# Attention and mixer kernel on one core: a fourth Strassen pair, earlier input sums, scores as two jobs, and a planner with new costs and rank offsets

## The chip, the cores and the metric

One NeuronCore of a Trainium2 chip runs the whole program in one launch. The metric is device microseconds of one execution. The kernel before took 565.9 us (median of 3 runs, 565.84 to 566.09). The execution that was profiled took 566.33 us.

## The reference

Causal attention over 4 batches, 12 heads, 448 positions and 64 channels a head, then a mixer on the attention's output, all in float32 (the weights come as float64):

```
x  = softmax(mask(q k^T / 8)) v            # 4 x 12 x 448 x 64, then 4 x 448 x 768
u  = x + (relu(x^T w_tok1) w_tok2)^T       # token mixing, 448 -> 256 -> 448
out = u + relu(u w_ch1) w_ch2              # channel mixing, 768 -> 1536 -> 768
```

Float32 accuracy is kept with split operands: each factor is held as a high and a low part, and a product is three matmuls (high by high, high by low, low by high).

## The kernel before, in words

The kernel first writes down jobs, then a planner (`Plan.emit`, L137) puts them into an order, and only that order is sent to the engines. A job has the engines that may do it with a cost in ns for each, the jobs that it needs, the buffers and PSUM banks that it holds, and a rank. The planner keeps a clock of its own: whenever an engine is free on that clock, it gets the ready job of the lowest rank whose buffers and banks are open; a job with a choice of engines goes where it would end first. Buffers of one name are a ring, and are given out strictly in the order in which the program asked for them. On the chip every engine then works through its list in order, and waits where a semaphore says so. When PE has nothing ready in the first 75 us of the planner's clock, a matmul without use (L602, the filler) is put in.

The stages:

1. Attention, by pairs of heads (24 pairs, 6 a batch). `load_pair` (L626) loads k, q and v with 11 DMA issues a pair. `prep` (L658) transposes k and q on VectorE into two `kq` buffers (five in all). `heads` (L672) has the scores as one PE job, `qk` (L689): 14 matmuls on 64 by 64 quarters of the array, 28 records in the trace, into four PSUM banks, which it and the four `prob` buffers have to be had together. Then come `low` (VectorE, minimum), `expo` (ScalarE), `guard` and `recip`, and `norm`. Pairs 0 to 11 turn the probabilities by PE (`by_tensor`, L759), pairs 12 to 23 by DMA (`by_dma`, L801), where `split` (L822) separates the 16-bit halves into the other `prob` buffer of each name. `values` (L863) multiplies with v on 128 by 64 halves of the array; `xturn` (L908) turns the result.
2. Token mixing, `tokens` (L959), in three parts a batch, with hidden values in `h1h` and `h1l` (one buffer each).
3. Channel mixing. The 1536 inner columns are 12 blocks of 128, in four quarters of three. `channels` (L1046) does one quarter for one or two batches: `up` (products with w_ch1), relu and its low part, then `down`, and `add` (L1120) puts the result onto `u` in place. `STAGES` (L274) says which quarter for which batches. A quarter for one batch is 108 matmuls of 448 columns. Batches 2 and 3 take blocks 3 to 8 together, in three pairs of blocks by Strassen's scheme: `mixtures` (L1152) makes four sums of the two batches' inputs for each of three row blocks, `combined` (L1247) makes the sums of the weights, and `group` (L1320) does the seven products, the sums of these, the relu and the downs. `mixtures` takes its buffers from attention once this is over; `combined` takes `u` buffers that earlier batches no longer need, and `wraw`.
4. `store` (L1490) turns a finished block of `u` on VectorE into a `kq` buffer and sends it with four DMA issues; `finish` (L1457) does the last block.

Before the change batches 2 and 3 already have quarter 0 added (for batch 2 in stage 4) when `mixtures` runs, so it has to rebuild batch 2's input from its two parts (`again`, L1210).

Of the kernel before, what the change touches and what calls it, by code (L numbers as in the profile page):

```python
# [19 lines left out]

class Slot:


    def __init__(self, ring):
        self.ring = ring
        self.index = ring.uses
        self.left = 0
        self.tile = None
        ring.uses += 1

    def take(self):
        self.ring.taken.append(self)
# [16 lines left out]
class Bank:  # L49


    def __init__(self, plan, kind, share):
        self.plan, self.kind, self.share = plan, kind, share
        self.left = 0
        self.bank = None

# [4 lines left out]
    def take(self):  # L61
        p = self.plan
        self.bank = p.banks.pop(0)
# [7 lines left out]
class Job:  # L71
    def __init__(self, order, costs, fn, rank, moved, lock=False):
        self.order, self.costs, self.fn, self.rank, self.moved, self.lock = order, costs, fn, rank, moved, lock
        self.waits = 0
        self.ready = 0.0
        self.after = []
        self.takes = []
        self.holds = []
# [4 lines left out]
class Plan:  # L83
# [7 lines left out]
    WINDOW, KEEP, WARM = 3400.0, 0.65, 75000.0  # L91
    LAG = {"pe": 230.0, "act": 150.0, "dve": 150.0, "pool": 150.0, "sp": 100.0}
    OWN = {"pe": 0.0, "act": 100.0, "dve": 130.0, "pool": 100.0, "sp": 100.0}
# [28 lines left out]
    def job(self, costs, fn, needs=(), holds=(), rank=0.0, moved=0.0, lock=False):  # L122

        j = Job(len(self.jobs), costs, fn, rank, moved, lock)
# [4 lines left out]
        for s in holds:  # L129
            if s.left == 0:  # L130
                j.takes.append(s)
            s.left += 1
# [4 lines left out]
    def emit(self):  # L137
        now = 0.0
        free = dict.fromkeys(self.ENGINES, 0.0)
        port = {"dve": 0.0, "pool": 0.0}  # L140
        dma = 0.0

        def until(j, e, t):
# [3 lines left out]
            return t + j.costs[e]  # L147
# [17 lines left out]
        while left:  # L165
# [3 lines left out]
            for e in self.ENGINES:  # L169
# [4 lines left out]
                while ready[e]:  # L174
# [4 lines left out]
                    open_ = all(s.open() for s in j.takes) and self.fits(j)  # L179
# [29 lines left out]
                end = until(pick, e, now)  # L209
                if e == "pool" or (e == "dve" and pick.lock):  # L210
                    port[e] = end
                free[e] = end
                if e == "pe":
                    self.spans.append((now, end))
                if pick.moved:
                    dma = end = max(end + 650.0, dma) + pick.moved
                    end += 800.0
                heapq.heappush(events, (end, 0, pick.order, pick))
# [25 lines left out]
def kernel(  # L244
# [72 lines left out]
    def act_ps(n):  # L317
        return 160.0 + 0.833 * n

    def act_sb(n):  # L320
        return 200.0 + 0.833 * n

    def dve1(n):
        return 150.0 + 1.04 * n

    def dve2(n):
        return 150.0 + 0.55 * n

    def pool1(n):
        return 230.0 + 0.85 * n  # L330

    def pool2(n):
        return 270.0 + 2.1 * n

    def pe(*ns):
        return sum(max(109.0, 0.458 * n) for n in ns)

    def move(n):
        return n / 290.0
# [45 lines left out]
    def narrow(n, shape, source, f, rank, needs=(), raw=None):  # L385
# [31 lines left out]
        j = plan.job({"sp": 520.0}, load, holds=[raw], rank=rank, moved=move(shape[0] * n * 8))  # L417
        j = plan.job({"act": act_sb(n)}, size, [j, *needs], [raw, f], rank)
# [5 lines left out]
    def token_weights():  # L424
        work = [(w_tok1, w1hi, w1lo, c, 0, DT) for c in range(NCH)]
        work += [(w_tok2, w2hi, w2lo, c, o, S // 2) for c in range(NM) for o in (0, S // 2)]
        for n, (src, hi, lo, c, o, w) in enumerate(work):
# [10 lines left out]
            a = narrow(w, [P, 1, w], source, f, TRANK, raw=slot(("wh", "wl")[n % 2]))  # L438
# [17 lines left out]
    def channel_weights(stage, o):  # L456
# [5 lines left out]
        size = P * NT * P * 4  # L462
        if stage < NQT:
            def source():
# [12 lines left out]
                {"sp": 520.0},  # L477
                lambda e: nc.sync.dma_start(out=scratch[m], in_=flat(f.tile)),
                got, [f], rank, moved=move(size),
            )  # L480
        else:
            got = [plan.job(
                {"sp": 520.0},
# [3 lines left out]
                [saved[m]], [f], rank, moved=move(size),  # L487
# [31 lines left out]
    def reread(sources, saves, rank):  # L519
# [7 lines left out]
        return f, plan.job({"sp": 520.0}, load, saves, [f], rank, moved=move(P * NT * P * 4))  # L527
# [37 lines left out]
    QUARTERS = ((0, 0, 6), (0, 1, 5), (1, 2, 4), (1, 3, 3), (0, 1, 1), (1, 3, 2), (1, 2, 0),  # L565
# [991 lines left out]
```

## Time and profile before

| | |
|---|---|
| median of 3 runs | 565.9 us |
| profiled execution | 566.33 us, of which span 564.6 us |
| PE busy | 548.2 us, 97% |
| DVE, ACT, POOL busy | 395.0, 304.7, 223.1 us |
| TensorE's granted clock | 1.00 in all 40 slices |
| chain that ended last | PE 90%, DMA issue queue of SP 3%, ACT 3%, DMA 2%, DVE 1% |
| filler matmuls (L602) | 55 |

The span is the time from the first to the last instruction; the rest of an execution's time lies around it. PE's busy time is a union of records whose ends are modelled, so a PE that looks busy can still have gaps between starts; distances between starts are the safer reading.

### The profile page before, as it was taken

Reading aid. Unit: us, or ns where it says so; the run is one execution under the profiler, and the core shown is the slowest. Engines: PE = TensorE matmul, PEld = TensorE weight load, DVE = VectorE, ACT = ScalarE, POOL = GpSimd, SP = SyncE. Lnnn points to the kernel's source line nnn. Section 1 sums busy time; section 2 is a strip of 40 time slices with the busy share of each in tenths; the row PEclk is TensorE's granted clock in tenths of the full one; section 3 lists DMA queues with packets and bytes.
Section 4 is the critical chain, followed back from the end, with each engine's and each line's share of the span. In section 5 each row is a group of like instructions: output and inputs, shape, how many; then the busy total and the mean of one; then the engine's idle time right before and its main releaser. Section 6 shows DMA issues by size and latency. Waiting matters only on the chain.

```text
span 564.6 us, 10295 instructions
## 1 busy us (share of the span) xinstructions
PE 548.2 (97%) x3512; PEld 473.5 (84%) x3512; DVE 395.0 (70%) x925; ACT 304.7 (54%) x746; POOL 223.1 (40%) x320
## 2 busy tenths in 40 slices
PE   8789999999999999999999999999999999999996
PEld 4467888878888988988988988988999998999995
DVE  4575868588777677778867687566576668677835
ACT  3678888787687566776667754674143120111010
POOL 2465675535352321430353621353356546232001
PEclk9999999999999999999999999999999999999999
DMA  6777647576988689789996766766221030312525
GB/s 112 157 154 149 155 104 174 161 180 150 197 224 190 149 203 204 177 222 200 217 217 132 151 111 122 148 126 127 62 74 56 29 111 2 111 55 86 126 57 99
DMA packets 230340, 77.37 MB, mean 137 GB/s; under 512 B 206544, under 2 KB 219024, under 8 KB 230288
## 3 DMA queue, kind: packets, MB, share of 16 engines
q1 hardware_dynamic: 217056, 74.99, 58.6%
q10 hardware_dynamic: 13232, 1.72, 1.8%
q8 instruction: 28, 0.46, 0.3%
q14 instruction: 24, 0.20, 0.1%
HBM read 49.15 MB, written 14.94 MB: 114 GB/s over the span
## 4 chain that ended last, share of the span: by engine, by line
PE 90%; SPq 3%; ACT 3%; DMA 2%; DVE 1%; issue 0%; POOL 0%; DVEq 0%; ACTq 0%
PE ps L1056 48%; PE ps L1444 8%; PE ps L882 7%; PE ps L1376 6%; PE ps L1007 5%; PE ps L974 5%; PE ps L695 5%; PE ps L781 3%; SPq L635 2%; PE ps L928 2%; DMA wl<-in_moe_w_tok_dram 1%; ACT prob L724 1%; SPq L400 1%; ACT pt L343 0%; DMA kq<-in_q_dram 0%
## 5 line engine op out<-in xcount | busy, mean ns | idle before, releaser
L1124 DVE TENSOR_TENSOR u<-ps,u 128x448 f32<-128x448 f32 x107 | 66.3, 622 | 47.1 <-PE ps L1056 33.6
L724 ACT ACTIVATE prob<-prob,stat 128x448 f32<-128x448 f32 (+6 forms) x168 | 84.0, 504 | 26.1 <-DVE stat L712 25.9
L345 POOL TENSOR_SCALAR prob<-prob,stat 128x448 f32<-128x448 f32 (+6 forms) x125 | 69.9, 572 | 39.7 <-DVE stat L746 36.7
L1056 PE MATMUL ps<-gh,wh 128*128 128x448 f32 x216 | 80.6, 373 | 0.0
L1056 PE MATMUL ps<-gh,wl 128*128 128x448 f32 x216 | 79.0, 366 | 0.0
L1056 PE MATMUL ps<-gl,wh 128*128 128x448 f32 x216 | 79.0, 366 | 0.0
L1056 PE MATMUL ps<-uh,wh 128*128 128x448 f32 x198 | 75.0, 379 | 0.0
L1056 PE MATMUL ps<-uh,wl 128*128 128x448 f32 x198 | 72.5, 366 | 0.0
L1056 PE MATMUL ps<-ul,wh 128*128 128x448 f32 x198 | 72.4, 366 | 0.0
L345 POOL TENSOR_SCALAR wh<-wf 128x768 fp32r<-128x768 f32 x27 | 23.1, 854 | 113.4 <-PE ps L1056 65.1
L712 DVE CUSTOM_DVE_ANT_0 prob<-ps,mask 128x448 f32<-128x448 f32 (+6 forms) x168 | 62.3, 412 | 0.3 <-PE ps L695 0.3
L743 POOL TENSOR_SCALAR stat<-stat 128x3 f32<-128x3 f32 (+1 forms) x43 | 13.3, 309 | 96.5 <-ACT prob L724 95.0
L882 PE MATMUL ps<-pt,vraw 128*64 128x448 f32 (+3 forms) x384 | 46.8, 386 | 1.4 <-ACT pt L343 1.4
L882 PEld LDWEIGHTS ps<-pt,vraw 128*64 128x64 f32 x384 | 25.4, 136 | 25.0 <-issue 14.0
L349 ACT COPY pt<-pt 128x512 uint16<-128x512 uint16 (+1 forms) x46 | 36.8, 875 | 15.5 <-DMA pt<-prob 15.4
L1056 PEld LDWEIGHTS ps<-gh,wh 128*128 128x128 f32 x216 | 40.6, 188 | 3.7
L1056 PEld LDWEIGHTS ps<-gl,wh 128*128 128x128 f32 x216 | 40.6, 188 | 3.5 <-DVE gl L1092 0.3
L1056 PEld LDWEIGHTS ps<-gh,wl 128*128 128x128 f32 x216 | 40.5, 188 | 3.2
L695 PEld LDWEIGHTS ps<-kq,kq 64*64 64x64 f32 x672 | 36.0, 132 | 8.3 <-issue 4.2
L695 PE MATMUL ps<-kq,kq 64*64 64x448 f32 (+6 forms) x672 | 41.8, 383 | 0.0
L354 DVE TENSOR_TENSOR wl<-wf,wh 128x768 fp32r<-128x768 f32 x35 | 35.9, 1033 | 8.5 <-ACT wh L343 4.9
L1056 PEld LDWEIGHTS ps<-uh,wh 128*128 128x128 f32 x198 | 37.2, 188 | 3.7
(144 smaller groups left out, 1224.2 us busy)
## 6 DMA issues: line engine op xcount, KB each, us to landing
wraw<-in_moe_w_ch_dram SPq DMA_DIRECT2D x24, 768.0 KB, 5.3
wf<-scratch SPq DMA_DIRECT2D x30, 384.0 KB, 3.2
scratch<-wf SPq DMA_DIRECT2D x24, 384.0 KB, 5.8
vraw<-in_v_dram SPq DMA_DIRECT2D x48, 96.0 KB, 2.4
out_dram<-kq SPq DMA_DIRECT2D x68, 56.0 KB, 1.8
kq<-in_k_dram SPq DMA_DIRECT2D x60, 56.0 KB, 3.9
kq<-in_q_dram SPq DMA_DIRECT2D x56, 56.0 KB, 2.5
gh<-in_k_dram SPq DMA_DIRECT2D x36, 56.0 KB, 2.3
```

Of the source, the lines that this page charges most:

```text
L345: eng[e].tensor_scalar(dst, src, scale, 0.0, op0=ALU.mult, op1=ALU.add)
L349: nc.scalar.copy(out, in_)
L354: eng[e].tensor_tensor(dst, a, b, op=ALU.subtract)
L695: nc.tensor.matmul(scores[r].tile[lanes, WHERE[c]:WHERE[c] + wide(c)], lhsT=qe.tile[LANES[j], c * QC:(c + 1) * QC], rhs=ke.tile[LANES[j], ...
L712: nc.vector.tensor_tensor_reduce(out=part(c, r), in0=ps.tile[:, WHERE[c]:WHERE[c] + wide(c)], in1=mask[:, S - wide(c):], scale=-SCALE, sca ...
L724: nc.scalar.activation(part(c, r), part(c, r), AF.Exp, bias=stat.tile[:, 0, AT[c]:AT[c] + 1], scale=-1.0, accum_out=stat.tile[:, 1, AT[c]: ...
L882: nc.tensor.matmul(ps.tile[LANES[j], c * QC:(c + nq) * QC], lhsT=s.tile[:, kb, j], rhs=view[:, o:o + nq, j], start=(kb == 0), stop=(n == 3),)
L974: nc.tensor.matmul(ps.tile[:, :PART], lhsT=w[:, c, m * P:(m + 1) * P], rhs=x.tile[:, c, :], start=(n == 0), stop=(n == len(work) - 1),)
L1056: nc.tensor.matmul(ps.tile[:, :S], lhsT=x.tile[:, at_:at_ + P], rhs=y, start=(n == 0 and i == 0), stop=(n + 1 == w[2] and i == 2),)
L1124: eng[e].tensor_tensor(u, ps.tile[:, :S], u, op=ALU.add)
L1376: nc.tensor.matmul(ps.tile[:, :S], lhsT=l()[:, t * P:(t + 1) * P], rhs=r, start=(t == 0 and n == 0), stop=(t == half - 1 and n == 2),)
L1444: nc.tensor.matmul(ps.tile[:, :S], lhsT=l.tile[:, t * P:(t + 1) * P], rhs=r.tile, start=(n == 0), stop=(n == 3 * len(fs) - 1),)
```

## The change

- **Strassen for a fourth pair.** Stage 5, quarter 3 (blocks 9, 10, 11) of batches 2 and 3, goes. Block 11 becomes a group of its own with plain products, and blocks 9 and 10 a pair by Strassen's scheme; both run ahead of the three pairs there were.
- **Sums of mixed inputs.** `mixtures` reads batch 2's and 3's `u` as the token mixing leaves it, so `again` goes, and every addition onto `u` of batches 2 and 3 now waits for the sums that read that block. The token weights' storage, free after the last token mixing, serves as further places for the sums; one `pt` buffer is given to the combined weights in place of a second `u` buffer.
- **Scores as two jobs**, one for two banks each, and with the 14 matmuls in another order: the two heads now alternate, head 0 on the upper and head 1 on the lower 64 rows of the array, both into the same bank.
- **Stores** use `h1h` and `h1l` instead of `kq`.
- **The planner**: costs of nearly all operations are changed; a DMA's time is modelled with a lead, a duration and the room in its ring; switching PE between quarters and the whole array costs 100 ns; from 30 us on the costs of ACT, DVE and POOL are taken 10% higher; transposes on PE don't count against the filler; and a table, `NUDGE`, adds an offset to the rank of 136 kinds of jobs (name and rank).

```diff
+NUDGE = {
+    "narrow.shift": {3.5: 18, 14: 6},
+    "token_weights.<lambda>": {3.5: -43},
+    "heads.expo": {0: 12, 2: -44, 10: 0.4, 12: 3, 14: -16, 24: 43, 26: 15, 32: 18.7, 44: 3},
+    "heads.<lambda>": {6: -19, 14: 38, 16: -43, 20: 17, 28: -7, 40: -10, 44: 3},
...
+    "group.down": {59.04: 9, 59.21: 14, 59.38: 45, 59.55: 5, 59.89: 12, 60.06: 5, 60.4: -8, 60.74: -19, 61.47: 3,
+        64.89: -8, 65.97: -6},
...
+}
-    WINDOW, KEEP, WARM = 3400.0, 0.65, 75000.0
-    LAG = {"pe": 230.0, "act": 150.0, "dve": 150.0, "pool": 150.0, "sp": 100.0}
+    LEAD, SWITCH, RING = 1400.0, 100.0, 128.0
+    SLACK, SETTLED = 1.1, 30000.0
+    WINDOW, KEEP, WARM = 3400.0, 0.7, 75000.0
+    LAG = {"pe": 200.0, "act": 145.0, "dve": 130.0, "pool": 80.0, "sp": 100.0}
...
+        rank = rank + NUDGE.get(name, {}).get(round(rank, 3), 0.0)
...
+                if e == "pe":
+                    end += self.SWITCH * (pick.tiled != tiled)
...
+                    while queued(e, end) + pick.ring > self.RING:
+                        end += 20.0
+                    start = max(now + self.LEAD, dma)
+                    dma = start + pick.moved
...
-    STAGES = ((0, (0,)), (1, (0, 1)), (2, (0, 1)), (3, (0, 1)), (0, (1, 2)), (3, (2, 3)), (0, (3,)))
+    STAGES = ((0, (0,)), (1, (0, 1)), (2, (0, 1)), (3, (0, 1)), (0, (1, 2)), (0, (3,)))
-    GROUPS = ((3, 4), (5, 6), (7, 8))
+    FIRST_GROUP = 5.0
+    SPAN = (0.34, 0.63)
+    GROUPS = ((11,), (9, 10), (3, 4), (5, 6), (7, 8))
...
     def act_ps(n):
-        return 160.0 + 0.833 * n
+        return 65.0 + 0.833 * n
...
-    QUARTERS = ((0, 0, 6), (0, 1, 5), (1, 2, 4), (1, 3, 3), (0, 1, 1), (1, 3, 2), (1, 2, 0),
-                (1, 1, 5), (1, 0, 6), (0, 3, 3), (0, 2, 4), (0, 3, 2), (0, 2, 0), (1, 1, 1))
+    QUARTERS = ((0, 0, 6), (1, 0, 6), (0, 1, 5), (1, 1, 5), (0, 1, 1), (1, 1, 1),
+                (0, 3, 3), (1, 3, 3), (0, 2, 4), (1, 2, 4), (0, 3, 2), (1, 3, 2), (0, 2, 0), (1, 2, 0))
...
-        holds = scores + probs + [ke, qe, stat]
-        m = plan.job({"pe": 1900.0}, qk, ready + [last_qk[0]], holds, rank)
-        last_qk[0] = m
+        made = {}
+        for rg, cost in zip(RG, (930.0, 740.0)):
+            holds = [x for r in rg for x in (scores[r], probs[r])] + [ke, qe, stat]
+            m = plan.job({"pe": cost}, lambda e, rg=rg: qk(e, rg), ready + [last_qk[0]], holds, rank, tiled=True)
+            last_qk[0] = m
+            made.update(dict.fromkeys(rg, m))
...
-                exps.append(plan.job({"act": 480.0 + 0.833 * wide(c)}, expo, [a], [probs[r], stat], rank))
+                exps.append(plan.job({"act": 277.0 + 0.857 * wide(c)}, expo, [a], [probs[r], stat], rank))
...
-        if b == B - 1:
-            ready.append(unmixed[t])
+        if b >= B - 2:
+            ready += unmixed[b, t]
...
-            p1, i1, e1 = again(t)
-            p2, i2, e2 = again(t + half)
-            x1, j1, f1 = mix("T1", t, p1, at(u3, t), ALU.subtract, [i1] + n3, [e1, u3])
-            mix("T3", t, p2, p1, ALU.subtract, [i1, i2], [e1, e2])
-            x2, j2, f2 = mix("T2", t, p2, x1, ALU.subtract, [i2, j1], [e2, f1])
-            x4, j4, f4 = mix("T4", t, at(u3, t + half), x2, ALU.subtract, [j2] + n3, [u3, f2])
-            unmixed[t], unmixed[t + half] = j1, j4
+            v = t + half
+            n2, m2, n3, m3 = u_whole[B - 2, t], u_whole[B - 2, v], u_whole[B - 1, t], u_whole[B - 1, v]
+            x1, j1, f1 = mix("T1", t, at(u2, t), at(u3, t), ALU.subtract, [n2, n3], [u2, u3])
+            _, j3, _ = mix("T3", t, at(u2, v), at(u2, t), ALU.subtract, [n2, m2], [u2])
+            x2, j2, f2 = mix("T2", t, at(u2, v), x1, ALU.subtract, [m2, j1], [u2, f1])
+            _, j4, _ = mix("T4", t, at(u3, v), x2, ALU.subtract, [m3, j2], [u3, f2])
+            unmixed[B - 2, t], unmixed[B - 2, v] = [j1, j3], [j2, j3]
+            unmixed[B - 1, t], unmixed[B - 1, v] = [j1], [j4]
...
-            spare.extend([slot("u"), slot("u"), slot("wraw")])
+            spare.extend([slot("u"), slot("pt"), slot("wraw")])
...
     def store(b, t, ready):
-        o = slot("kq")
+        o = slot(("h1h", "h1l")[t % 2])
...
-    for stage in range(len(STAGES) - 2):
+    mixtures()
+    for stage in range(len(STAGES) - 1):
         channels(stage)
-    mixtures()
-    channels(len(STAGES) - 2)
-    for number in range(len(GROUPS)):
-        group(number, 6.0 + number * 0.63)
+    at = FIRST_GROUP
+    for number, fs in enumerate(GROUPS):
+        group(number, at)
+        at += SPAN[len(fs) - 1]
     channels(len(STAGES) - 1)
```

## Rows read from the trace of the kernel before

**Rows 1.** The page: span, busy time and share of each engine.

```profile
span 564.6 us, 10295 instructions
...
PE 548.2 (97%) x3512; PEld 473.5 (84%) x3512; DVE 395.0 (70%) x925; ACT 304.7 (54%) x746; POOL 223.1 (40%) x320
```

**Rows 2.** Windows: length; busy PE, PEld, DVE, ACT, POOL (count); clock, DMA share, GB/s.

```profile
0.00:20.00 20.00, 15.65 (x116) 8.81 (x120) 8.77 (x37) 8.90 (x25) 7.07 (x29) 1.00 0.69 137
20.00:40.00 20.00, 16.60 (x150) 11.75 (x144) 14.04 (x51) 14.74 (x51) 12.02 (x24) 1.00 0.74 140
40.00:60.00 20.00, 18.14 (x173) 14.12 (x176) 13.25 (x49) 17.25 (x56) 10.97 (x23) 1.00 0.72 143
60.00:403.80 343.80, 342.76 (x2332) 297.10 (x2325) 252.71 (x634) 235.29 (x571) 131.45 (x193) 1.00 0.74 167
538.00:564.60 26.60, 22.26 (x110) 19.69 (x108) 12.03 (x20) 2.49 (x4) 3.43 (x3) 1.00 0.40 76
```

**Rows 3.** Chain that ended last, in time: start, us, what.

```profile
403.76 49.45 PE ps L1056 x243
```

**Rows 4.** Waits of PE, whole span: who for whom, us, times, longest.

```profile
PE ps L1444 <- DVE gl L1312: 1.4, 1, 1.4
```

**Rows 5.** PE by line, 0 to 60 us: count, busy us, mean ns.

```profile
L602 PE MATMUL ps<-mask 128*128 128x512 bf16 x55 | 15.6, 422 | 1.4 <-POOL mask L364 1.4
```

**Rows 6.** PE timeline, 0 to 60 us: start, length, operation, count.

```profile
7.08 1.74 PE L695 MATMUL ps<-kq,kq 64*64 64x448 f32 x28
...
21.04 1.95 PE L882 MATMUL ps<-pt,vraw 128*64 128x448 f32 x16
...
55.28 1.95 PE L882 MATMUL ps<-pt,vraw 128*64 128x448 f32 x16
57.16 1.09 PE L781 MATMUL ps<-across_ident,prob 128*128 128x128 f32 x8
```

**Rows 7.** Waits of ACT, 0 to 60 us.

```profile
ACT wf L403 <- DMA wl<-in_moe_w_tok_dram: 3.9, 2, 2.5
```

**Rows 8.** PE timeline, 290 to 300 us, around one pair's scores.

```profile
296.52 0.37 PE L1056 MATMUL ps<-ul,wh 128*128 128x448 f32 x1
296.73 0.36 PE L1056 MATMUL ps<-uh,wl 128*128 128x448 f32 x1
297.02 1.74 PE L695 MATMUL ps<-kq,kq 64*64 64x448 f32 x28
298.69 0.47 PE L1056 MATMUL ps<-uh,wh 128*128 128x448 f32 x1
299.00 0.36 PE L1056 MATMUL ps<-ul,wh 128*128 128x448 f32 x1
```

**Rows 9.** ACT timeline, 286 to 298 us, splits of the pair before.

```profile
286.97 1.03 ACT L349 COPY prob<-prob 128x1024 uint16<-128x1024 uint16 x1
...
294.43 1.04 ACT L349 COPY prob<-prob 128x1024 uint16<-128x1024 uint16 x1
```

**Rows 10.** DVE timeline, 286 to 298 us, its other two splits.

```profile
289.81 0.69 DVE L351 COPY prob<-prob 128x1024 uint16<-128x1024 uint16 x1
...
292.67 0.69 DVE L351 COPY prob<-prob 128x1024 uint16<-128x1024 uint16 x1 [0.39 <-POOL prob L345]
```

**Rows 11.** Line 1494 (transpose of a finished block): count, ns min/median/max.

```profile
L1494 DVE STREAM_TRANSPOSE kq<-u x23: 602/645/648, 344.4 to 558.4; 128x448 f32<-128x448 f32 x23
```

**Rows 12.** SP timeline, 380 to 470 us: output issues.

```profile
384.61 4.39 SPq L1498 DMA_DIRECT2D out_dram<-kq  x8
```

**Rows 13.** DMA issues by line: count, KB each, us to landing.

```profile
out_dram<-kq SPq DMA_DIRECT2D x68, 56.0 KB, 1.8
```

**Rows 14.** ACT timeline, 436 to 460 us: first split of combined weights.

```profile
437.18 0.83 ACT L343 ACTIVATE u<-wf 128x768 fp32r<-128x768 f32 x1
```

**Rows 15.** DVE timeline, 451 to 460 us: last split of combined weights.

```profile
453.87 0.96 DVE L354 TENSOR_TENSOR wraw<-wf,wraw 128x768 fp32r<-128x768 f32 x1
```

More of the change, by code (lines that the diff above doesn't have):

```diff
@@ L141, in emit, with queued @@
         dma = 0.0
+        tiled = False
+        rings = {e: [] for e in self.ENGINES}
+        def queued(e, t):
+            return sum(n * min(1.0, max(0.0, (b - t) / (b - a))) for a, b, n in rings[e])
         def until(j, e, t):
@@ L146, in until @@
                 t = max(t, port["dve" if e == "pool" else "pool"])
-            return t + j.costs[e]
+            return t + j.costs[e] * (self.SLACK if now >= self.SETTLED and e not in ("pe", "sp") else 1.0)
         ready = {e: [] for e in self.ENGINES}
@@ L178, in emit @@
                         continue
-                    open_ = all(s.open() for s in j.takes) and self.fits(j)
+                    open_ = all(s.got for s in j.joins) and all(s.open() for s in j.takes) and self.fits(j)
                     if open_ and len(j.costs) > 1:
@@ L383, with narrow @@
     CRANK, CSTEP, CLEAD, WLEAD, TRANK = 2.0 * H - 6.0, 6.0, -9.0, 6.0, 3.5
-    def narrow(n, shape, source, f, rank, needs=(), raw=None):
+    def narrow(n, shape, source, f, rank, needs=(), raw=None, issues=1):
         raw = raw or slot("wraw")
@@ L415, in join @@
             )
-        j = plan.job({"sp": 520.0}, load, holds=[raw], rank=rank, moved=move(shape[0] * n * 8))
-        j = plan.job({"act": act_sb(n)}, size, [j, *needs], [raw, f], rank)
+        moved, ring = (3000.0, 60) if n > 2 * P else (800.0, 16)
+        j = plan.job({"sp": 530.0 * issues}, load, holds=[raw], rank=rank, moved=moved, ring=ring)
+        j = plan.job({"act": 115.0 + 0.92 * n}, size, [j, *needs], [raw, f], rank)
         j = plan.job({"dve": dve2(n)}, shift, [j], [f], rank, lock=True)
@@ L525, in load @@
             nc.sync.dma_start(out=sources(to)[0], in_=sources(to)[1])
-        return f, plan.job({"sp": 520.0}, load, saves, [f], rank, moved=move(P * NT * P * 4))
+        return f, plan.job({"sp": 530.0}, load, saves, [f], rank, moved=1200.0)
     def up_block(fb, rank):
@@ L687, in heads, with qk @@
         scores = [share("s") for _ in ROUND]
-        def qk(e):
-            for r in range(len(ROUND)):
+        def qk(e, rg):
+            for r in rg:
                 bank(scores[r])
@@ L835, in turn @@
                 nc.sync.dma_start_transpose(out=t16.tile[:, r], in_=both.tile.bitcast(U16))
-            a = plan.job({"sp": 1250.0}, turn, [a], [both, t16], rank, moved=1570.0)
+            a = plan.job({"sp": 1310.0}, turn, [a], [both, t16], rank, moved=1900.0, ring=73)
             def merge(e, r=r):
@@ L888, in pv @@
                         )
-            cost = sum(52.0 + QC * STEPS[n][3] / 0.6 for n in part)
-            prev = plan.job({"pe": cost}, pv, js + pdone + [prev], [ps, s, pt, u], rank)
+            cost = sum(10.0 + QC * STEPS[n][3] / 0.6 for n in part) + 70.0 * part[0]
+            prev = plan.job({"pe": cost}, pv, js + pdone + [prev], [ps, s, pt, u], rank, tiled=True)
         def evac(e):
@@ L905, in values @@
         first = [u_ready[b, 0]] if t else []
-        u_ready[b, t] = plan.job({"act": 200.0 + act_ps(S), "dve": 140.0 + dve1(S)}, evac, [prev] + first, [ps, u], rank)
+        u_ready[b, t] = plan.job({"act": 110.0 + act_ps(S), "dve": 120.0 + dve1(S)}, evac, [prev] + first, [ps, u], rank)
     def xturn(g):
@@ L1135, in add @@
         begun[b, t] = times + 1, last
-        if times + 1 == (NQT if b < 2 else 2 + len(GROUPS)):
+        if times + 1 == (NQT if b < 2 else sum(b in bs for _, bs in STAGES) + len(GROUPS)):
             store(b, t, last)
@@ L1175, in home, with of, behind @@
             return x.tile[:, o]
+        def of(h):
+            return [] if h[0] is None else [h[0]]
+        def behind(h):
+            return mixed_by if h[0] is None else claimed([h[0]])
         def mix(name, t, a, b, op, needs, holds):
@@ L1324, in group @@
         half = NT // 2
-        span = 0.34 if len(fs) == 1 else 0.63
+        span = SPAN[len(fs) - 1]
         total = float(36 * len(fs))
```

154 lines of the change are left out of this document (96 added, 58 removed).

## The prediction

> **What bounds the kernel now.** I read the page's busy times first, then windows by stage, then the chain, then the waits of PE. The page [rows 1] has PE busy in 97% of the span and the next engine in 70%, but the first 60 us are another stage than the rest. In the windows [rows 2] PE is busy 342.76 of 343.80 us from 60 us to the end of attention, at a granted clock of 1.00 (the 2.4 GHz level), while in the first 60 us it is busy 50.4 of 60, and 15.6 us of that are 55 filler matmuls without use [rows 5]. So there are two kinds of time: from 60 us on whatever takes matmuls off PE or puts idle time between them moves the end one for one; before that PE has 9.6 us idle and 15.6 us of filler, 25.2 us in all, and what counts is how soon the attention's chains feed it. The sum below is made against the profiled execution, 566.33 us (span 564.6 and 1.7 around it); the median of the runs is 0.43 us less, which I take off at the end.
>
> **The change part by part.**
>
> *Fourth Strassen pair.* Quarter 3 of two batches was 216 matmuls of 448 columns. Now block 11 has 36 up and 36 down, blocks 9 and 10 have 7 products of 9 and 72 down, 207 in all: 9 fewer. In the long stretch after attention 243 matmuls took 49.45 us [rows 3], 0.2035 us each. That is -1.83 us, with no doubt but whether PE stays fed. VectorE gets more to do there (12 more additions, 7 sums of products, 4 sums of weights), but it is idle for a third of such a stretch.
>
> *The stall at the first Strassen group.* Its downs waited 1.4 us for VectorE's last low part [rows 4], since no other matmul was ready. Now block 11's downs (36 x 0.2035 = 7.3 us) can lie there, if they aren't used up earlier (below). I take -0.8, bounds -1.4 and 0.
>
> *The planner's costs and offsets in the first 60 us.* Of the 25.2 us, 7.1 lie ahead of the first scores, which start at 7.08 us [rows 6] after loads and transposes that stay. Pair 0 then needs until 21.04 us for its values; two pairs' probabilities fit, so that stretch can't be filled, and I leave it 5 us. What remains, 13 us, is the most that a better order can give. It can be got only if the others keep pace: ScalarE is busy 14.74 and 17.25 us from 20 to 40 and from 40 to 60 us [rows 2], so 8.0 us idle, and 3.9 us of its waiting is for the token weights' DMA [rows 7], a wait at which everything behind it on ScalarE, the next pair's exponentials too, stands still. A planner that knows when a load lands would put those exponentials first. The new costs are nearer to the records: a mean exponential (256 columns) took 504 ns [rows 1] and is planned at 496 instead of 693, and a transfer has its lead and its duration. Half of the bound is -6.5 us; bounds -13 and 0 (a worse order costs as well, but nothing in the costs points that way). The rule for fillers gives more of them rather than fewer, at 0.2 us each, and only where PE has nothing else; I count nothing for them.
>
> *Small waits after 60 us.* 1.04 us idle are left up to 403.8 [rows 2]; a new order may take some and make others: -0.7, bounds -1.0 and +1.0.
>
> *Scores as two jobs.* If the second half follows the first at once, nothing changes but the order of the quarters. If other matmuls come between, a pair pays for a second visit to the quartered array. Its price by rows: matmuls start 0.21 us apart, but 0.29 before the scores and 0.31 after their first successor [rows 8], so 0.09 going in and 0.10 coming out. The scores take 1.67 us (297.02 to 298.69) [rows 8] and the values 1.88 us (55.28 to 57.16) [rows 6], for 896 columns in each quarter and 1024 in each half; with the same fixed part that gives 1.64 ns a column and 0.20 us fixed. And the halves are uneven (512 and 448 columns in the fullest quarter against 896), 64 columns or 0.10 us. Together 0.5 us a visit. In the DMA half of attention a visit of its own is likely: the scores at 297.02 come right behind the last of the four splits of the pair before (294.43 + 1.04), while the first two of these ended at 290.5 [rows 9, 10], so that two of the four buffers are free some 5 us earlier, and the planner gives PE to the lowest rank that is ready. It does charge itself 0.1 us for a switch. I take 6 of 24 pairs, +3.0; bounds 0 and 24 x 0.5 = 12.
>
> On the page "TensorEngine Tiling (Array Packing)", section "Key Properties", the Trainium skill says that a change of tiling mode drains TensorE. The 0.09 and 0.10 us of rows 8 are what such a drain would look like here, and by the rule every pair that is split pays it, so the sum would lie towards the end of 12.
>
> *Sums of mixed inputs, stores, and what waits for them.* Six sums on POOL go, off the path. But three waits are added. (1) Additions of stage 4 onto batch 2 wait for sums that need batch 3's first blocks; behind such an addition on VectorE stand the attention's operations, and in front of it the matmul's PSUM bank stays taken. (2) The sums wait for buffers that attention frees at its end, and they now have less time: from the end of token mixing at 403.8 us there are 27 matmuls of stage 4 (243 - 216 [rows 3]), 36 up and 36 down of block 11, 20.1 us, and two products without sums (3.7 us), where there were 49.45 us. (3) Stores use two single buffers that come free only when the last token mixing is done, and batch 0's `u` buffer goes to the combined weights only after its six stores. A transpose takes 0.645 us [rows 11], four issues 2.2 us (8 in 4.39 [rows 12]) on SP alone, a landing 1.8 us [rows 13]. The fifth and sixth store need a buffer back, the sixth after four times four issues: 0.65 + 8.8 + 1.8 + 0.65 = 11.9, so 415.7 us. The combined weights took 17.6 us before, from 437.18 to 454.83 [rows 14, 15], in no hurry. At that pace the third product could start at 433.3, while PE's other work ends at 403.8 + 20.1 + 3.7 = 427.6: 5.7 us idle. In a hurry (a split 0.83 + 0.96 twice, five steps of some 0.6 between) it is 6 to 7 us, done by 422.5, and nothing waits. I take +1.0; bounds 0 and 13 (5.7, and 7.3 more if block 11's downs are put behind the products).
>
> *The end.* Batch 3's stores come every nine matmuls, 1.83 us, on two buffers whose round is 0.645 + 2.2 + 1.8 = 4.6 us against 3.66. The fifth starts 2 x 1.0 us late, but it had slack to the last block's own tail (4.3 us of PE idle after 538 [rows 2]). +0.5, bounds 0 and +2.
>
> Sum: -1.8 - 0.8 - 6.5 - 0.7 + 3.0 + 1.0 + 0.5 = -5.3, so 561.0 for an execution like the profiled one and 560.6 for the median.
>
> **The rivals.**
>
> *The early stretch gives all it can* (-13 instead of -6.5): 554.1. For it: 25 us of PE's time are lost there, and 8 us of ScalarE's idle could be used by moving evacuations to VectorE, which has 12.7 us free from 20 to 60 [rows 2]. Against it: 11 loads a pair on one queue, and two pairs of buffers.
>
> *The early stretch gives nothing*: 567.1, no change. For it: the plan is the same greedy one, and an engine's list runs in order whatever its costs were. Against it: the wait in rows 7 is one of order.
>
> *Combined weights too late* (slower). Place: between the last token mixing and the first new products. Price: 13 us with block 11's downs behind the products, in place of the +1.0: 572.6. It decides once PE idles there for over 7.5 us (5.3 + 1.0 + the 1.1 that can be told from no change). For it: a chain of stores, buffer, splits and sums that had 49 us of cover and has 20. Against it: the hurried chain ends 5 us before it is needed.
>
> *The heads take turns.* The new order has the upper and the lower half of the rows write one PSUM bank at the same time; the old order kept them on different banks but for short ends. If they took turns, 896 columns would become 1792: +1.47 us a pair, 35 us in all, 596. Against it: the values, which never have two row halves, take 1.88 / 1024 = 1.84 ns a column with everything in, and the scores 1.67 / 896 = 1.86, although in the old order too both halves write the second bank for part of the block (0.2 us by the column counts). The Trainium skill's page "TensorEngine Tiling (Array Packing)", section "Restrictions and Gotchas", says this rule outright: different row tiles cannot access the same PSUM bank at once. By it the 596 would hold; the rate in rows 6 and 8 gives no sign of it.
>
> **How the numbers follow.** Forecast 0.61 (alone 555.5 to 564.7: half of the early term's spread, and 0 to 12 pairs split), all of the early bound 0.15, nothing early 0.11, weights late 0.10, turns 0.03. A measurement tells 0.2%, 1.1 us, from no change. Faster: 0.59 of the forecast's 0.61 and 0.15, so 0.74. Same: 0.02 of the forecast and 0.07 of "nothing early", 0.09. Slower: 0.04 of that, 0.10 and 0.03, 0.17. The range from 550.5 to 568 leaves out the 0.13 of the slow cases and little below.
>
> **What would show it.** In the trace after: 207 matmuls in place of 216, and no PE wait for VectorE's low part at the first Strassen downs. In the first 60 us fewer fillers and less idle: PE's lost time at 18.7 instead of 25.2 us, and ScalarE no longer waiting 3.9 us for token weights. Score records in blocks of 14 with other matmuls between, in about six pairs, each whole pair 1.67 us when together. Idle of PE between 404 and 430 us at most 1 us. I am wrong if PE idles for several us there, if the scores' blocks grow to some 3 us, or if the lost time up to 60 us is still 25.

## The result and the profile after

The changed kernel takes 561.22 us (median of 5 runs, 560.12 to 562.97) against 566.09 us for the kernel before on the same chip; the ratio is 0.9916, 95% interval [0.9892, 0.9941]. Run again beside the last experiments it took 561.66 us, ratio 0.9917 [0.9903, 0.9931]. The prediction was 560.6 us; the measured time lies in its range, and the kernel is faster, as forecast. The profiled execution took 561.22 us, with a span of 559.4.

The page of the changed kernel, first its span and busy times [rows 1], then the exponentials of part 5, whose mean is 502 ns; the last line is that of the exponentials before (504 ns), the figure in the prediction's argument on costs:

```profile
span 559.4 us, 10287 instructions
...
PE 548.0 (98%) x3492; PEld 463.6 (83%) x3492; DVE 407.4 (73%) x951; ACT 311.0 (56%) x783; POOL 194.5 (35%) x279
...
L798 ACT ACTIVATE prob<-prob,stat 128x448 f32<-128x448 f32 (+6 forms) x168 | 83.7, 502 | 20.7 <-DVE stat L786 20.1
...
L724 ACT ACTIVATE prob<-prob,stat 128x448 f32<-128x448 f32 (+6 forms) x168 | 84.0, 504 | 26.1 <-DVE stat L712 25.9
```

The changed kernel by windows, with the columns of [rows 2]:

```profile
0.00:20.00 20.00, 17.73 (x137) 9.18 (x139) 10.88 (x48) 12.20 (x38) 10.14 (x37) 1.00 0.67 133
20.00:40.00 20.00, 18.29 (x161) 12.89 (x159) 14.24 (x49) 18.46 (x64) 12.30 (x24) 1.00 0.76 154
40.00:60.00 20.00, 18.70 (x178) 14.59 (x173) 14.67 (x56) 17.46 (x56) 9.65 (x20) 1.00 0.69 136
60.00:200.00 140.00, 140.00 (x1075) 112.93 (x1075) 110.25 (x314) 121.91 (x329) 57.85 (x90) 1.00 0.83 177
200.00:400.00 200.00, 200.00 (x1205) 174.64 (x1205) 152.04 (x323) 118.50 (x263) 59.26 (x75) 1.00 0.72 161
400.00:440.00 40.00, 39.88 (x197) 36.53 (x196) 27.54 (x42) 6.58 (x11) 10.35 (x10) 1.00 0.27 71
```

Its fillers up to 60 us, by line [rows 5]:

```profile
L670 PE MATMUL ps<-mask 128*128 128x512 bf16 x44 | 13.3, 439 | 1.4 <-POOL mask L432 1.4
```

PE is now busy 54.72 of the first 60 us instead of 50.39, and 13.3 us of that are fillers instead of 15.6. Idle and filler together fell from 25.2 to 18.6 us, where the prediction had 18.7. From 60 to 400 us PE never stands, and the 5.7 us of idle that the prediction works out near 430 us for combined weights made without hurry are not there: 0.12 us idle from 400 to 440.

All waits of PE in the changed kernel (who for whom; us, times, longest) [rows 4], and the longest of ScalarE up to 60 us, in the changed kernel and then in the kernel before [rows 7]:

```profile
PE ps L766 <- DVE kq L736: 1.7, 1, 1.7
PE ps L670 <- POOL mask L432: 1.4, 1, 1.4
PE ps L855 <- POOL prob L413: 1.3, 1, 1.3
PE ps L766 <- DVE stat L820: 0.9, 1, 0.9
PE ps L1514 <- DVE gl L1382: 0.4, 1, 0.4
```
```profile
ACT prob L798 <- DVE stat L786: 5.8, 3, 4.6
...
ACT prob L724 <- DVE stat L712: 7.0, 2, 6.2
```

The wait for VectorE's low part ahead of the Strassen downs is 0.4 instead of 1.4 us. ScalarE's 3.9 us for the token weights are gone, and the wait for VectorE's minima, its longest in both kernels, went from 7.0 to 5.8 us; it is busy 48.1 us of the 60, against 40.9.

PE's timeline in the changed kernel, around a whole pair of scores (line 766), and around one in two parts [rows 8]:

```profile
249.17 0.37 PE L1133 MATMUL ps<-uh,wl 128*128 128x448 f32 x1
249.47 1.75 PE L766 MATMUL ps<-kq,kq 64*64 64x448 f32 x28
251.15 0.67 PE L1083 MATMUL ps<-w2hi,h1h 128*128 128x448 f32 x2
```
```profile
261.99 0.36 PE L1133 MATMUL ps<-uh,wl 128*128 128x448 f32 x1
262.28 1.09 PE L766 MATMUL ps<-kq,kq 64*64 64x448 f32 x12
263.31 1.95 PE L956 MATMUL ps<-pt,vraw 128*64 128x448 f32 x16
265.19 0.97 PE L766 MATMUL ps<-kq,kq 64*64 64x256 f32 x16
266.09 0.47 PE L1133 MATMUL ps<-gh,wh 128*128 128x448 f32 x1
266.40 0.36 PE L1133 MATMUL ps<-gl,wh 128*128 128x448 f32 x1
```

A whole pair takes 251.15 - 249.47 = 1.68 us, as before. In two parts it takes 1.03 + 0.90 = 1.93: 0.25 us more. In the records 17 of the 24 pairs are in two parts, 11 of them after 60 us. Once, at 69.75, the second part of one pair and the first of the next stand together and take 1.68 us, so 16 extra visits are paid, 10 of them after 60 us. The way in (0.29 instead of 0.20) and out (0.31) stands once here, since the values lie between the parts.

**The bill.** I use one more reading: PE's lost time, which is fillers plus what passes from the start of one group of matmuls to the start of the next beyond the group's usual pitch (0.2035 us for 448 columns [rows 3], 1.67 us for a pair's scores [rows 8]). Unlike busy time it sees gaps under overlapping records.

| profiled execution | 0-60 us | 60-400 us | last channel matmul to end | span |
|---|---|---|---|---|
| before | 24.8 | 8.0 | 5.38 | 564.55 |
| after | 19.6 | 8.75 | 6.47 | 559.43 |

The span fell by 5.1: -1.8 for the 9 matmuls, -5.2 before 60 us, +0.7 up to 400, +0.1 after, +1.1 at the end. A trace is a single execution: two of the changed kernel lost 19.6 and 20.3 us before 60 us, and two of the run tail below, whose engines have the same lists up to 500 us, 18.2 and 18.9. So differences of up to 2 us there can be scatter.

### The profile page after: what moved, and what is told of

It is laid out like the page before. It is cut to its first block, busy times and chain, and to the rows that moved or that the text cites. A ratio compares the mean times of both kernels' runs of the same rounds, so it can differ in the third digit from the quotient of the medians.

```text
span 559.4 us, 10287 instructions
## 1 busy us (share of the span) xinstructions
PE 548.0 (98%) x3492; PEld 463.6 (83%) x3492; DVE 407.4 (73%) x951; ACT 311.0 (56%) x783; POOL 194.5 (35%) x279
## 4 chain that ended last, share of the span: by engine, by line
PE 90%; SPq 4%; DVE 2%; DMA 2%; issue 1%; POOL 0%; ACT 0%; ACTq 0%; DVEq 0%; POOLq 0%
PE ps L1133 39%; PE ps L1514 11%; PE ps L1446 8%; PE ps L956 7%; PE ps L766 6%; PE ps L1083 5%; PE ps L1050 5%; PE ps L855 3%; SPq L703 2%; PE ps L1002 2%; PE ps L1423 1%; DMA gl<-in_q_dram 1%; DVE gl L1382 1%; DVE u L1201 1%; SPq L716 1%
## 5 line engine op out<-in xcount | busy, mean ns | idle before, releaser
L1133 PE MATMUL ps<-gh,wh 128*128 128x448 f32 x180 | 66.9, 372 | 0.0
L1133 PE MATMUL ps<-gl,wh 128*128 128x448 f32 x180 | 65.9, 366 | 0.0
L1133 PE MATMUL ps<-gh,wl 128*128 128x448 f32 x180 | 65.9, 366 | 0.0
L413 POOL TENSOR_SCALAR prob<-prob,stat 128x192 f32<-128x192 f32 (+6 forms) x106 | 56.5, 546 | 23.9 <-DVE stat L820 23.0
L1133 PE MATMUL ps<-uh,wh 128*128 128x448 f32 x162 | 60.4, 373 | 0.0
L1133 PE MATMUL ps<-ul,wh 128*128 128x448 f32 x162 | 59.3, 366 | 0.0
L1133 PE MATMUL ps<-uh,wl 128*128 128x448 f32 x162 | 59.3, 366 | 0.0
L766 PE MATMUL ps<-kq,kq 64*64 64x64 f32 (+6 forms) x672 | 47.1, 388 | 2.6 <-DVE kq L736 1.7
L411 ACT ACTIVATE wh<-wf 128x768 fp32r<-128x768 f32 x12 | 10.1, 844 | 56.2 <-PE ps L1133 22.5
L1377 ACT ACTIVATE gh<-kq 128x448 fp32r<-128x448 f32 x16 | 8.7, 575 | 58.0 <-DVE kq L1476 58.0
L1514 PE MATMUL ps<-gl,wh 128*128 128x448 f32 x108 | 39.8, 369 | 0.5 <-DVE gl L1382 0.4
L1514 PE MATMUL ps<-gh,wl 128*128 128x448 f32 x108 | 39.6, 366 | 0.0
L1514 PE MATMUL ps<-gh,wh 128*128 128x448 f32 x108 | 39.5, 366 | 0.0
```

The source lines that it names most:

```text
L413: eng[e].tensor_scalar(dst, src, scale, 0.0, op0=ALU.mult, op1=ALU.add)
L766: nc.tensor.matmul(scores[r].tile[lanes, WHERE[c]:WHERE[c] + wide(c)], lhsT=qe.tile[LANES[j], c * QC:(c + 1) * QC], rhs=ke.tile[LANES[j], ...
L1133: nc.tensor.matmul(ps.tile[:, :S], lhsT=x.tile[:, at_:at_ + P], rhs=y, start=(n == 0 and i == 0), stop=(n + 1 == w[2] and i == 2),)
L1514: nc.tensor.matmul(ps.tile[:, :S], lhsT=l.tile[:, t * P:(t + 1) * P], rhs=r.tile, start=(n == 0), stop=(n == 3 * len(fs) - 1),)
```

## The experiments

All ratios are against the kernel before on the same chip. "Without offsets" means an empty table `NUDGE`.

**tail: the last batch's stores.** The end after the last channel matmul got 1.1 us longer. Line 1564 is the store's transpose; VectorE in the changed kernel:

```profile
552.14 0.64 DVE L1564 STREAM_TRANSPOSE h1l<-u 128x448 f32<-128x448 f32 x1
553.36 0.62 DVE L1201 TENSOR_TENSOR u<-ps,u 128x448 f32<-128x448 f32 x1 [0.59 <-PE ps L1133]
554.39 0.65 DVE L1564 STREAM_TRANSPOSE h1h<-u 128x448 f32<-128x448 f32 x1 [0.41 <-DMA out_dram<-h1h]
```

The last block is ready at 553.98, but its transpose waits until 554.39 for a store to leave `h1h`; four issues and a landing follow. Batch 3's stores went back to `kq`, and the one offset that delays this block's downs was taken out, two edits at once:

```diff
-        76.84: 15},
+        },
...
-        o = slot(("h1h", "h1l")[t % 2])
+        o = slot(("h1h", "h1l")[t % 2] if b < B - 1 else "kq")
```

> The changed kernel, but batch 3's stores use kq again and the offset that puts block 4's downs behind block 5's is gone; only the last 20 us differ. My theory: from the last matmul of the channel mixing to the end of the span the changed kernel took 6.5 us (before: 5.4), since the last block goes through a store of four issues and its transpose waits for a buffer. Here it is 5.4 again and the time 1.1 us below the changed kernel (560.1). Rival: the end is set by the last DMA's landing whatever the order, and the 6.5 us stay (561.2).

Measured 559.04 us (558.43 to 561.66), 0.9891 [0.9874, 0.9908]. The end of its VectorE:

```profile
550.75 0.65 DVE L1564 STREAM_TRANSPOSE kq<-u 128x448 f32<-128x448 f32 x1
551.92 0.69 DVE L1536 TENSOR_TENSOR u<-ps,u 128x224 f32<-128x224 f32 x2 [0.52 <-PE ps L1133]
552.84 0.76 DVE L413 TENSOR_SCALAR kq<-ps 112x256 f32<-112x256 f32 x2 [0.23 <-PE ps L1542]
```

No store is waited for, and `finish` (L1536) does the last block again. From the last channel matmul to the end it is 5.39 us. Of the two edits the buffers are enough to explain the end: in struct_only and no_offsets below, which have no offsets, `finish` comes late too, but with stores in `h1h` the end took 6.66 and 6.82 us, and a last transpose waited 0.37 and 0.33 us for a store to leave; with stores in `kq` (struct_kq, costs_only) it took 5.44 and 5.40. The offset alone was not run.

**tail_again and after_again**, the same two kernels on one chip:

> The kernel of the run tail (the last batch's stores in kq, offset 76.84 taken out), on one chip with the changed kernel. Theory: 1.1 to 1.4 us below it. Rival: the difference between two calls was the chip's, and here it is under 0.5 us.

> The changed kernel itself, as the measure for the three others on the same chip: 561.2 us by its own runs.

Measured 559.12 (558.32 to 562.42), 0.9890 [0.9871, 0.9909], and 561.66 us. Last channel matmul to end: 5.39 and 6.45, so 1.06 us in both pairs of profiles. The medians lie 2.2 and 2.5 us apart, the ratios 0.25% and 0.27% (1.4 and 1.5 us). What lies beyond 1.1 us in the profiled executions is mostly in the first 60 us (18.2 and 18.9 us lost against 19.6 and 20.3), where the edit changes no engine's list: scatter. So 1.06 us is shown, and the intervals of the ratios overlap a little.

**no_offsets: the changed kernel with the table empty.**

```diff
-NUDGE = {
...
-}
+NUDGE = {}
```

> The changed kernel with an empty table of offsets; all costs and all of the structure stay. My theory (the prediction's): better costs keep engines from standing at a wait while other work is ready, so at least half of the early gain stays: PE's lost time up to 60 us (fillers and idle; 24.8 us before, 19.6 after) is at most 22 us, the time about 563.5. Rival: the offsets alone made the early gain, the lost time is 24 us or more and the time 566 or above.

Measured 566.77 us (564.64 to 568.46), 1.0017 [1.0005, 1.0029]: no gain is left. The theory, that costs alone give most of it, missed by 3 us. Lost: 22.7 us before 60 (the theory had at most 22, the rival 24 or more), 12.1 from 60 to 400 us. Its windows around a stall:

```profile
50.00:54.00 4.00, 1.69 (x13) 1.25 (x12) 2.51 (x11) 2.22 (x9) 1.67 (x4) 0.98 0.81 204
54.00:58.00 4.00, 4.00 (x26) 2.19 (x28) 1.97 (x7) 2.37 (x8) 0.98 (x3) 0.59 0.81 164
```

PE is busy 1.69 of 4 us, and right behind it the granted clock is 0.59 in the mean: at 0.50, the 1.2 GHz level, from 53.84 to 57.26 us by its records.

**costs_only: the new planner and costs on the old work**, without offsets; the old stages, groups and order of quarters are put back, scores one job, `mixtures` as before, stores in `kq`:

```diff
-    GROUPS = ((11,), (9, 10), (3, 4), (5, 6), (7, 8))
+    GROUPS = ((3, 4), (5, 6), (7, 8))
...
-        for rg, cost in zip(RG, (930.0, 740.0)):
+        for rg, cost in (((0, 1, 2, 3), 1670.0),):
```

> The kernel before with the new planner and costs and no offsets: three Strassen pairs, sums rebuilt, scores as one job in the old order, stores in kq. My theory: the early gain of the costs alone, -2.5 us or more, so 563.5 or below. Rival (the offsets or the structure are the source): 565.5 to 567.

Measured 565.17 us (564.55 to 567.03), 0.9992 [0.9982, 1.0002]: -0.8 us in the medians, and not told from no change; the theory missed, and the rival's range lies just above. Its first 60 us, with the columns of [rows 2]:

```profile
0.00:60.00 60.00, 55.77 (x469) 38.00 (x471) 37.10 (x139) 47.11 (x153) 30.44 (x74) 1.00 0.70 140
```

What the prediction expected of costs does happen there: ScalarE no longer waits for the token weights, and is busy 47.1 us instead of 40.9. But the lead isn't kept. Lost before 60 us are 22.6 us instead of 24.8; counted matmul by matmul, this run is 4.5 us ahead of the kernel before at 40 us, 1.8 at 60 and 0.5 at 70, and fillers up to 60 us rose from 55 to 71. So the costs, on which the prediction's largest term was argued, give about an eighth of it to the time. What eats the lead from 40 us on is open.

**no_off_one: without offsets, scores as one job**, in the new order of quarters:

```diff
-        for rg, cost in zip(RG, (930.0, 740.0)):
+        for rg, cost in (((0, 1, 2, 3), 1670.0),):
```

> As no_offsets, but scores as one job of 14 matmuls (in the new order). My theory: each pair whose halves were apart paid 1.025 + 0.905 us for 1.68, and two changes of tiling more; the score blocks take 24 x 1.68 again, 4 to 5 us less, and the time falls from 566.8 to about 562.5. Rival: the halves bought that back, because the first pairs' exponentials start earlier; PE's lost time up to 60 us (22.7 in no_offsets) grows by as much, and the time stays at 566 or rises.

Measured 564.03 us (562.92 to 564.85), 0.9966 [0.9955, 0.9977]. Against no_offsets the two jobs cost 2.7 us, not the theory's 4 to 5. Before 60 us it lost 23.4 us against 22.7, so the halves may buy 0.7 back there, as the rival says, though that is within the scatter. Against costs_only the structure (Strassen, sums, stores), together with the new order of quarters, gives 1.1 us.

**struct_only: the old planner and costs on the new structure**, scores one job in the old order:

```diff
-    GROUPS = ((3, 4), (5, 6), (7, 8))
+    GROUPS = ((11,), (9, 10), (3, 4), (5, 6), (7, 8))
...
-        if b == B - 1:
-            ready.append(unmixed[t])
+        if b >= B - 2:
+            ready += unmixed[b, t]
```

> The kernel before with the old planner and costs, and the fourth pair, the early sums, the token weights' storage, the pt buffer and the stores in h1h and h1l; scores as one job in the old order. My theory: 9 matmuls less (-1.8), the first group's stall gone (-0.8), the end later (+1.1): 564.6, with the first 60 us as before (24.8 us lost). Rival 'combined weights too late': PE idles for several us between 404 and 430 us, and the time is 568 or more. Rival 'structure is the source': 562 or below.

Measured 569.28 us (568.82 to 570.23), 1.0066 [1.0053, 1.0079]: slower than before, where the theory had 564.6. The first 60 us are as before (24.6 us lost), but PE lost 5.8 us from 435 to 444. VectorE from 435 to 441 us, and the waits of PE from 400 to 460 us; line 1492 is the store's transpose, 1404 a sum of products, 1129 an addition onto `u`, 356 and 1310 are low parts of weights and of hidden values, 1442 the downs:

```profile
435.08 1.23 DVE L1129 TENSOR_TENSOR u<-ps,u 128x448 f32<-128x448 f32 x2
436.22 0.61 DVE L1404 TENSOR_TENSOR kq<-kq,ps 128x448 f32<-128x448 f32 x1
436.75 0.64 DVE L1492 STREAM_TRANSPOSE h1l<-u 128x448 f32<-128x448 f32 x1
437.31 0.58 DVE L1404 TENSOR_TENSOR kq<-kq,ps 128x448 f32<-128x448 f32 x1
437.82 0.94 DVE L356 TENSOR_TENSOR wl<-wf,wh 128x768 fp32r<-128x768 f32 x1
438.68 1.68 DVE L1310 SCALAR_TENSOR_TENSOR gl<-kq,gh 128x448 fp32r<-128x448 f32 x3
```
```profile
PE ps L1442 <- POOL wl L356: 2.4, 1, 2.4
PE ps L1442 <- DVE gl L1310: 1.4, 1, 1.4
```

The time is that of the rival "too late" (568 or more), but its place and cause are not. The combined weights aren't late. VectorE is: its list has two additions and a store's transpose among the sums that the downs need, and it works through them without a pause (busy 3.81 of the 4 us from 434 to 438, and all of 438 to 440). The transpose doesn't hold it up: no wait of VectorE for a store is longer than 0.3 us there. The two waits make 3.8 us; the rest is lost behind them, where TensorE's granted clock was 0.50 from 439.83 to 443.25 us and matmuls of 448 columns stood 0.37 us apart. That the order is the cause is read from the trace; no run changes it alone.

**struct_kq: the same with the stores in `kq`.**

```diff
-        o = slot(("h1h", "h1l")[t % 2])
+        o = slot("kq")
```

> As struct_only, but stores use kq (five buffers) as before. In struct_only PE stood still for 5.8 us between 434 and 440 us while VectorE waited with a store's transpose for the DMA out of h1h, with the sums of Strassen products behind it. My theory: the two single buffers are that stall's cause; without them it is gone and the time falls from 569.3 to about 563.5, below the kernel before. Rival: the new products' operands are late (PE also waited 2.4 us for a low part of weights on POOL), the stall stays and the time is 568 or more.

Measured 576.65 us (575.93 to 578.09), 1.0185 [1.0168, 1.0202]. The theory, that another place for the stores heals it, fell. It had read the stall as a wait of VectorE for the DMA out of `h1h`, which the trace of struct_only doesn't show. PE's waits from 400 to 460 us, and the piece of the chain that ended last ahead of the longer one (start, us, what):

```profile
PE ps L1442 <- POOL wh L347: 5.2, 1, 5.2
PE ps L1374 <- POOL u L347: 2.7, 1, 2.7
```
```profile
444.02 3.59 DMA wf<-scratch
447.76 1.11 POOL wh L347
```

Two things are late. The combined weights (`u`, 2.7 us): batch 0's stores stand behind the sums in the ring of `kq`, and the weights need the buffer that these stores free. And the ordinary weights of the downs (`wh`, 5.2 us): their load could be issued only at 444.02, when SP was through with 48 issues of stores, which it had been at since 415. PE lost 15 us in all, with the granted clock at 0.50 behind both. Under the old planner, then, the change's stores in `h1h` and `h1l` are worth some 7 us, while tail shows that batch 3 is better without them.

**off_early and off_late: 30 of the offsets alone (ranks up to 12, the first seven pairs), or the other 106.** For one entry of the table, in off_early and then in off_late:

```diff
-    "heads.expo": {0: 12, 2: -44, 10: 0.4, 12: 3, 14: -16, 24: 43, 26: 15, 32: 18.7, 44: 3},
+    "heads.expo": {0: 12, 2: -44, 10: 0.4, 12: 3},
```
```diff
-    "heads.expo": {0: 12, 2: -44, 10: 0.4, 12: 3, 14: -16, 24: 43, 26: 15, 32: 18.7, 44: 3},
+    "heads.expo": {14: -16, 24: 43, 26: 15, 32: 18.7, 44: 3},
```

> The changed kernel with the offsets of ranks up to 12 alone (30 of 136: the seven first pairs and what belongs to them). All offsets together were worth 5.2 to 5.6 us, and PE's lost time fell by 3.2 us before 60 us and by 3.4 us from 60 to 400 us. Theory A, the two halves are independent and early offsets act early: 563 to 564.5 us, lost time before 60 us back at 19 to 20.5 us, from 60 to 400 us still 11 to 12.5. Rival B, offsets only fit the plan that all of them together make: 565.5 us or more.

> The changed kernel with the offsets of ranks above 12 alone (106 of 136). Theory A, halves independent: 563 to 564.5 us, lost time before 60 us about 22.7 us as without offsets, from 60 to 400 us 8.5 to 9.5. Rival B, they fit only the plan that the early ones leave, and an order tuned to another plan is no better than none: 566 us or more, with 11 us or more lost from 60 to 400 us.

Measured: off_early 564.95 us (562.88 to 570.83), 0.9998 [0.9971, 1.0025], lost 19.6 and 11.5 us; off_late 580.32 us (579.37 to 581.71), 1.0257 [1.0241, 1.0272], lost 21.3 and 24.8. For the early ones theory A holds in the lost time, but the profiled execution (562.91 us) is among the fastest of twelve; the median is just above its range, with a wide scatter that I can't explain. For the late ones rival B holds by far: with the early ones they take off 3.3 us (564.95 to 561.66), without them they add 13.6 (566.77 to 580.32). PE in off_late, where most of that is lost: a wait for the transposed k and q from 155 to 185 us, and a window behind it:

```profile
PE ps L757 <- DVE kq L727: 2.4, 1, 2.4
```
```profile
165.00:175.00 10.00, 7.34 (x28) 4.68 (x30) 7.79 (x23) 9.76 (x29) 2.73 (x8) 0.66 0.99 226
```

**one_searched and early_searched: one job again, all offsets new.** If the two jobs cost 2.7 us, one job with offsets of its own should beat tail. Both have tail's stores and a new table, found by trial of offsets against the planner's clock (616 and 646 entries); early_searched keeps two jobs for the first six pairs:

```diff
-        for rg, cost in zip(RG, (930.0, 740.0)):
+        for rg, cost in (((0, 1, 2, 3), 1670.0),):
```
```diff
-        for rg, cost in zip(RG, (930.0, 740.0)):
+        for rg, cost in (zip(RG, (930.0, 740.0)) if g < 6 else (((0, 1, 2, 3), 1670.0),)):
```

> The changed kernel with scores as one job, batch 3's stores in kq, and a table of offsets found anew for this program on the planner's own clock; all else as in the changed kernel. My theory: offsets are worth 5 to 6 us in any structure, and scores in halves only cost (2.7 us without offsets), so this is the 564.0 of no_off_one less 5 to 6 and less 1.1 at the end: 557 to 558, below the changed kernel and below 'tail' (559.0). Rival: the offsets need the halves, whose early start is what they exploit; then it is 561 or above.

> As one_searched, but the scores of the first six pairs stay two jobs (offsets found anew from the changed kernel's). My theory: the first pairs' halves cost at most 6 x 0.45 us and may shorten the first chains: 557 to 559. Rival (halves are what shortens the first 60 us): 2 us below one_searched, with PE's lost time up to 60 us less by as much.

Measured 560.96 us (559.52 to 563.64), 0.9908 [0.9888, 0.9928], and 560.91 (560.65 to 561.06), 0.9906 [0.9891, 0.9920]. Both theories missed: neither beats tail, and they are not apart. Of early_searched's rival the part on lost time held (18.9 us before 60 against 23.2), the part on the time didn't; the two tables differ as well, so the halves aren't shown to be the reason. one_searched lost only 6.3 us from 60 to 400 us, less than any other, but 23.2 before 60. Three engines of one_searched, in order VectorE, GpSimd, PE:

```profile
46.28 0.65 DVE L757 STREAM_TRANSPOSE kq<-gl 128x448 f32<-128x448 f32 x1 [2.66 <-DMA gl<-in_q_dram]
46.85 0.59 DVE L1112 TENSOR_TENSOR u<-ps,u 128x448 f32<-128x448 f32 x1
47.36 0.16 DVE L841 RECIPROCAL stat<-stat 128x3 f32<-128x3 f32 x1
```
```profile
47.69 1.55 POOL L434 TENSOR_SCALAR prob<-prob,stat 128x448 f32<-128x448 f32 x3 [5.33 <-DVE stat L841]
```
```profile
48.38 0.65 PE L876 MATMUL ps<-ident,prob 128*128 128x128 f32 x4 [3.35 <-POOL prob L434]
48.97 2.38 PE L787 MATMUL ps<-kq,kq 64*64 64x448 f32 x28
```

The planner gives out only what is ready on its own clock, so it had this load of q landed; on the chip it was late. VectorE stood 2.66 us at its transpose, and a reciprocal that had nothing to do with it stood behind; GpSimd waited for that, and PE for GpSimd, 3.35 us. Behind the idle time the granted clock was 0.50 from 49.92 to 53.34 us, and the 28 scores took 51.28 - 48.97 = 2.31 us instead of 1.68. early_searched, against tail, lost 0.7 us more before 60, 1.1 less from 60 to 400 and 2.5 more behind that.

## Why the prediction was right, point by point

- **Fourth pair: -1.83 predicted.** 207 matmuls stand in place of 216. By time, structure and quarter order gave -1.1 us under the new planner (no_off_one against costs_only), for -1.83 - 0.8 + 1.0 + 0.5 = -1.1 in the prediction's terms; that the sums agree is luck, since the end alone was mis-sized by 0.6. Under the old planner the same structure costs 3.3 us (struct_only).
- **Stall at the first Strassen group: -0.8.** The wait fell from 1.4 to 0.4 us.
- **The first 60 us: -6.5, "half of the bound".** The size held: -6.6 by the prediction's own measure, -5.2 by starts, which count the six pairs in two parts there (6 x 0.25 = 1.5 us). The reason failed in the main. "The new costs are nearer to the records" was to carry it. The costs do remove the wait for the token weights, but most of the lead is lost again by 70 us, and in time the costs carry -0.8 us (costs_only). The offsets carry 5.6 us (no_offsets to after), on both sides of 60 us: lost time 22.7 to 19.6 before, 12.1 to 8.75 after. The prediction had put costs and offsets into one term and argued only from the first. In time costs and offsets together make -0.8 - 5.6 = -6.4, close to what it had put down, but for the whole kernel and not for its first 60 us: luck. Why the offsets help, beyond less lost time, no run takes apart.
- **Small waits after 60 us: -0.7.** Without the scores' parts (10 x 0.25 = 2.5 us) the lost time there went from 8.0 to 6.25: -1.8. By busy time only 1.04 us were there to win; the rest is gaps that only distances between starts show.
- **Scores as two jobs: +3.0 as 6 pairs at 0.5.** 17 pairs are in two parts, 16 extra visits at 0.25 each and mostly no second way in and out, since the planner often puts the parts against the values: 78 changes between the whole array and its quarters or halves became 88. That is 16 x 0.25 = 4.0 us; in time +2.7 without offsets (no_offsets against no_off_one). Count and price were both wrong, and the errors nearly cancel.
- **Sums and waits: +1.0, bounds 0 and 13.** In the changed kernel nothing of it shows, as the hurried chain had it: ScalarE's splits of the combined weights [rows 14, 15] are at 414.33 and 415.63:

```profile
414.33 0.85 ACT L411 ACTIVATE u<-wf 128x768 fp32r<-128x768 f32 x1
415.63 0.85 ACT L411 ACTIVATE wraw<-wf 128x768 fp32r<-128x768 f32 x1 [0.46 <-DVE wf L1354]
```

  Losses of that size do occur under the old planner, 5.8 us and with `kq` 15. But none of the 5.8 and only 3.5 of the 15 (2.7 and 0.8) are waits for the combined weights; the prediction didn't have VectorE's order, the load behind stores on SP, and the lower clock behind each stall. With the new planner and no offsets (no_off_one) the 5.8 us are gone; which part of the planner saves them I haven't separated.
- **The end: +0.5, bounds 0 and 2.** It was +1.1. The prediction had the buffer's round, 4.6 against 3.66 us, and gave it slack to the last block's own tail. The slack wasn't there, with or without offsets: the end took 6.66 us in struct_only, 6.82 in no_offsets and 6.47 in the changed kernel, each with a last transpose that waits for `h1h`.
- **The rivals.** "Early stretch gives nothing" comes near to costs_only, where little of the early lead is left by 70 us; it isn't what the changed kernel does. "The heads take turns" is refuted: 1.68 us a whole pair with both row halves writing one bank throughout (in different partitions), where turns would add 1.47. The Trainium skill ("TensorEngine Tiling (Array Packing)", section "Restrictions and Gotchas") says that different row tiles cannot access the same PSUM bank at once; as a limit of rate this trace contradicts it.

In sum the terms -1.8, -6.7 (first 60 us without the scores' parts), -1.8, +4.0, +0.1 and +1.1 give the span's -5.1, for a forecast of -5.3. The total is better than its parts, and that is luck.

**Best version:** tail, 559.04 and 559.12 us (ratios 0.9891 and 0.9890), below both kernels in the medians; of its lead on the changed kernel 1.06 us is explained.

## What to carry to other kernels

Separate a plan's data from its tuning before giving a gain to either: a table of offsets fits one plan, and a part of it can be far worse than none (+13.6 us). With engines that work through a list in order, ask of each instruction what stands behind it. In one_searched an operation that was ready stood behind a transpose whose load hadn't landed; in struct_only sums that PE needed stood behind additions and a store's transpose that nobody waited for, and in struct_kq a load of weights behind 48 issues of stores. A work-saving change can need its buffers moved with it: under the old planner the same nine matmuls fewer came out at 569.3 us with one place for the stores and at 576.7 with the other.

## What the runs showed of the hardware

- A second visit to the quartered array costs 0.25 us in the scores themselves, and no further 0.19 us when the values lie next to it (262.28 to 266.40 us above).
- Behind a stall of PE its granted clock was at the 1.2 GHz level for a few us: 53.84 to 57.26 in no_offsets (2.3 us at a wait), 49.92 to 53.34 in one_searched (3.35), 167.39 to 174.22 in off_late (2.4, and more waits behind it), 439.83 to 443.25 in struct_only (2.4 and 1.4). In the kernels before and after it was 1.00 through the last matmul.
- A transpose into a buffer whose store hasn't landed yet stops VectorE until it has: 0.41 us at 554.39 in the changed kernel, 1.12 at 430.92 in struct_kq. A landing in the chain that ended last needn't be such a stop: in struct_only that chain holds 1.99 us of one (434.18 to 436.17), during which VectorE was at work.
